# The last block's output: four quarters summed by VectorE out of PSUM and stored as each is ready, the last one from two DMA queues

## The chip, the core and the metric

The kernel runs on one core of a Trainium2 chip. The metric is the device time of one execution in microseconds. The profiler gives, beside that time, the span from the first to the last instruction and a record of every instruction, DMA packet and semaphore. In what follows TensorE is PE (its weight loads are PEld), VectorE is DVE, ScalarE is ACT, GpSimd is POOL and SyncE is SP. SP computes nothing: it issues DMAs.

## The reference

Two stages run one after the other: attention that keeps the 32 largest scores of each row, and a gated feed-forward block on its result.

```python
scores = q @ k.T / sqrt(64)                      # 8 batches, 8 heads, 576 x 576
kth    = 32nd largest of each row
scores = where(scores >= kth, scores, -1e9)
attn   = exp(scores - max); attn /= sum + 1e-9
x      = (attn @ v) as (4608, 512)               # heads side by side
g      = x @ w_gate; val = x @ w_val             # 512 -> 1536
out    = (g * sigmoid(g) * val) @ w_out          # 1536 -> 512, (4608, 512) float32
```

## The kernel before

**Attention** is cut into units, one for a batch, a tile of 128 query rows (64 in the last) and a pair of heads. `scores` multiplies on PE, `select` finds the 32nd largest on DVE by rounds of MAX8 and MATCH_REPLACE8 (L339, L343), `penalize` (L361, POOL) and `weigh` (L370, ACT) form the exponentials, `turn` (L397) transposes them on PE and `values` (L426) multiplies by v. The loop over units at L718 keeps several units in flight and gives the feed-forward work out in pieces between them.

**Feed-forward** work is done in 18 blocks of 256 token rows (`BLK`) by the generator `feed(kb)`. It is ready when the attention rows that it needs are. A block forms `h`, the gated hidden values, in six steps of two 256-wide products each (L480). PE fills a PSUM bank; ACT reads it (L505 to L507, L512); POOL multiplies (L508, L513). When the units are used up, the rest of the work is done by `while piece(): pass` (L775), so the last block runs with no attention beside it.

**The output product** of each block but the first is made with a fast scheme of seven products instead of eight: `quarter(i, ps)` runs the i-th product, six matmul steps at L566 into a PSUM tile of 128 x 256. The order is 1, 7, 5, 6, 2, 4, 3. POOL prepares the operands: L573, L581, L586 and, for quarter 3, L614. `a` (products 5 and 7) and `b` (products 1 and 6) are copies in SBUF, made by ACT at L593 and L600 and summed up on POOL with `tt` (L552, in `sum_up`). The output tile `o` has 128 partitions, two row tiles t = 0 and 1, and 512 columns, so it has four parts of 128 x 256:

- t = 1, right: finished early, from sums of `a` and `b` alone;
- t = 0, left: product 2 plus `b[:, 0]`; ACT copies the bank (L624), POOL adds (L552);
- t = 1, left: product 4 plus `a[:, 1]`;
- t = 0, right: product 3 plus `a[:, 0]`.

Products 4 and 3 go into the two halves of one PSUM tile, `x_ps2`. After product 3, `rest_x` copies both halves by one ACT instruction of 128 x 512 (L636), `stores` adds `a` to both by one POOL instruction of 128 x 512 (L552), and then `store` sends the two row tiles.

`store(o, g0)` (L457) issues DMAs for 128 rows of the output. Since a row of the tile and a row of `out` are not in the same order, it splits the rows where the order breaks; in the last block each row tile gives two DMAs of 64 rows by 2 KB, so the block gives four, all from SP's queue.

**What sets the order.** Copies and POOL sums are put into the lists `on_act` and `on_pool`, and `flush` issues them at places in the loop. At the end every engine's instructions are tied into the order in which they were written (L781 to L794), so each engine runs its own list strictly in that order. PSUM is two pools: five banks for attention and three (`ps_f`) for the feed-forward block, taken in turn.

Of the kernel before, what the change touches and what calls it, by code (L numbers as in the profile page):

```python
# [9 lines left out]
ALU = mybir.AluOpType  # L10
FP32 = mybir.dt.float32
# [4 lines left out]
P = 128  # L16
# [4 lines left out]
BLK = 256  # L21
# [6 lines left out]
def kernel(  # L28
# [37 lines left out]
    nc = tc.nc  # L66
    B, H, S, D = q.shape
    DM, DFF = w_gate.shape
# [8 lines left out]
    NBLK = B * S // BLK  # L77
# [11 lines left out]
    ps_f = ctx.enter_context(tc.tile_pool(name="ps_f", bufs=3, space=PSUM))  # L89
# [355 lines left out]
            done[kb] += n_c  # L445
            at += n_c

    def store(o, g0):

        at = g0  # L450
        while at < g0 + P:
            b, c = divmod(at, S)
            j, p0 = divmod(c, P)
            n = min(g0 + P - at, S - c, P - p0)
            r0 = b * S + (c if j == J else J * p0 + j)
            dst = out[r0 : r0 + n, :] if j == J else out[r0 : r0 + J * (n - 1) + 1 : J, :]
            nc.sync.dma_start(dst, o[at - g0 : at - g0 + n, :])  # L457
            at += n

    on_act, on_pool = [], []  # L460

    def flush(queue):
        while queue:
            queue.pop(0)()

    def feed(kb):
# [50 lines left out]
        o = ffn.tile([P, 2, DM], FP32, tag="o", name="o", bufs=1)  # L517
        if plain:
            for t in range(2):
                ps = ps_f.tile([P, DM], FP32, tag="f", name="o_ps")  # L520
                for m in range(MC):
                    need(4 * MS + m + 1)
                    if m == 6:
                        flush(on_act)
                        flush(on_pool)
                    nc.tensor.matmul(  # L526
                        ps[:],
                        hs[m // 2][:, m % 2, t * P : (t + 1) * P],
                        wo[:, m, :],
                        start=(m == 0),  # L530
                        stop=(m == MC - 1),
                    )
                    if m == MC - 1:

                        def finish(ps=ps, t=t):
                            nc.scalar.copy(o[:, t, :], ps[:])
                            store(o[:, t, :], kb * BLK + t * P)

                        on_act.append(finish)
                        if t == 1:  # L540
                            plain_done.append(True)
                    if m % 2 == 1:
                        yield 1
            return
        while len(T[3]) < MQ:
            next(weight)
        DH = DM // 2
        y_ps = ps_f.tile([P, 2, DH], FP32, tag="f", name="y_ps")
        x_ps = ps_f.tile([P, 2, DH], FP32, tag="f", name="x_ps")

        def tt(out, in0, in1):
            nc.gpsimd.tensor_tensor(out, in0, in1, ALU.add)  # L552

        def quarter(i, ps):
            for m in range(MQ):
                s, r = m // 2, m % 2
                lhsT = {
                    1: lambda: hs[s][:, r, first],
                    2: lambda: hs[s + MS // 2][:, r, first],
                    3: lambda: hs[s][:, r, late],  # L560
                    4: lambda: hs[s + MS // 2][:, r, late],
                    5: lambda: hs[s][:, r, late],
                    6: lambda: s32[:, m],
                    7: lambda: s32[:, m],
                }[i]()
                nc.tensor.matmul(  # L566
                    ps, lhsT, T[i][m], start=m == 0, stop=m == MQ - 1
                )
                if m % 3 == 2:
                    yield 0.75  # L570
# [19 lines left out]
        a = ffn.tile([P, 2, DH], FP32, tag="gv", name="p57", bufs=3)  # L590
# [6 lines left out]
        b = ffn.tile([P, 2, DH], FP32, tag="gv", name="p16", bufs=3)  # L597
# [22 lines left out]
        y_ps2 = ps_f.tile([P, DH], FP32, tag="f", name="y_ps")  # L620
        yield from quarter(2, y_ps2[:])

        def rest_y():
            nc.scalar.copy(o[:, 0, 0:DH], y_ps2[:])  # L624
            on_pool.append(lambda: tt(o[:, 0, 0:DH], o[:, 0, 0:DH], b[:, 0]))

        on_act.append(rest_y)
        x_ps2 = ps_f.tile([P, 2, DH], FP32, tag="f", name="x_ps")
        yield from quarter(4, x_ps2[:, 1])
# [5 lines left out]
        def rest_x():  # L635
            nc.scalar.copy(middle, x_ps2[:])  # L636

            def stores():
                tt(middle, middle, a[:])
                for t in range(2):  # L640
                    store(o[:, t, :], kb * BLK + t * P)

            on_pool.append(stores)
# [7 lines left out]
    def piece():  # L651

        if len(on_act) > 1:
            flush(on_act)
        if len(on_pool) > 1:
            flush(on_pool)
        while True:
            if not current:
                if not todo or done.get(todo[0], 0) < NHP * BLK:
                    return 0  # L660
                flush(on_act)
                flush(on_pool)
                current.append(feed(todo.pop(0)))
            cost = next(current[0], 0)
            if cost == 0:
                current.pop()
                continue
            return cost
# [156 lines left out]
```

## Time and profile before

| | |
|---|---|
| median of 4 runs | 1838.76 us (1837.98 to 1840.82) |
| the profiled execution | 1839.38 us |
| its span | 1837.6 us |
| PE busy | 1707.3 us, 93% of the span |
| DVE, ACT, POOL busy | 88%, 65%, 55% of the span |
| DMA | 59.65 MB, mean 32 GB/s |
| mean granted TensorE clock | 0.964 |

The profiled execution's own time is 1.8 us more than its span. In the rows of the profile, `L566` is a line of the kernel, an `x12` behind a row is the number of instructions merged into it, and `[4.81 <-PE x_ps L566]` says that the engine had stood idle for 4.81 us until a PE instruction of that line ended. A `q` behind an engine's name (`SPq`) is its sequencer: there a DMA issue, a drain or a semaphore wait takes its time.

### The profile page before, as it was taken

What the parts mean: (1) busy time and instruction counts of PE and PEld (TensorE: products, weight loads), DVE (VectorE), ACT (ScalarE), POOL (GpSimd) and SP (SyncE); (2) the same over time, 40 slices, a digit from 0 to 9 for tenths busy, and PEclk for the clock granted to TensorE, in tenths of its full rate; (3) what the DMA queues carried; (4) which work ended last, traced back from release to release, by engine and by line L of the source; (5) the groups of instructions that cost most, each with busy time, mean ns of one, the idle gap of its engine ahead of it and who ended that gap; (6) DMA issues with size and microseconds to landing.
All of it is one profiled execution on the core that took longest, in us unless ns stands there. A gap on an engine that the chain in (4) does not pass through costs nothing.

```text
span 1837.6 us, 30517 instructions
## 1 busy us (share of the span) xinstructions
PE 1707.3 (93%) x10756; PEld 1409.0 (77%) x10756; DVE 1620.8 (88%) x3405; ACT 1202.7 (65%) x2943; POOL 1012.4 (55%) x932
## 2 busy tenths in 40 slices
PE   3438989899999989999999999999999999999998
PEld 2326668777788878887888878888788878888887
DVE  7999999999999879997999989998999989998400
ACT  5667776677666667676767676767776766675431
POOL 3556746645555545655464646564556554646444
PEclk7678999999999999999999999999999999999999
DMA  7322221000300021000300012000300011000000
GB/s 188 97 85 92 59 66 26 12 1 18 77 1 12 1 67 27 12 1 14 73 19 1 13 40 54 1 12 2 74 19 12 1 36 32 1 12 12 1 13 12
DMA packets 109145, 59.65 MB, mean 32 GB/s; under 512 B 88512, under 2 KB 96704, under 8 KB 108992
## 3 DMA queue, kind: packets, MB, share of 16 engines
q1 hardware_dynamic: 107936, 57.44, 12.1%
q8 instruction: 85, 1.39, 0.3%
q14 instruction: 68, 0.56, 0.1%
q10 hardware_dynamic: 1056, 0.26, 0.1%
HBM read 48.23 MB, written 9.44 MB: 31 GB/s over the span
## 4 chain that ended last, share of the span: by engine, by line
PE 82%; DVE 3%; POOL 2%; ACT 2%; issue 2%; DMA 0%; POOLq 0%; ACTq 0%; SPq 0%
PE f L480 39%; PE x_ps L566 9%; PE av L426 8%; PE etps L397 7%; PE s L318 7%; PE y_ps L566 6%; PE s L304 2%; PE av L417 1%; DVE m L339 1%; PE kqps L273 1%; DVE rest L343 1%; PE o_ps L526 1%; POOL e L361 1%; POOL p L552 0%; ACT e L370 0%
## 5 line engine op out<-in xcount | busy, mean ns | idle before, releaser
L339 DVE MAX8 m<-rest 128x8 f32<-128x576 f32 x864 | 613.6, 745 | 2.2
L361 POOL TENSOR_TENSOR e<-e,sc 128x1152 f32<-128x1152 f32 (+1 forms) x160 | 382.7, 2392 | 78.4 <-DVE e L349 72.7
L343 DVE MATCH_REPLACE8 rest<-m,rest 128x576 f32<-128x576 f32 x576 | 423.5, 741 | 0.0
L480 PE MATMUL f<-xT,wg 128*128 128x256 f32 x1728 | 401.6, 382 | 0.0
L480 PE MATMUL f<-xT,wv 128*128 128x256 f32 x1728 | 399.1, 382 | 0.0
L480 PEld LDWEIGHTS f<-xT,wg 128*128 128x128 f32 x1728 | 323.0, 190 | 62.6 <-issue 21.0
L480 PEld LDWEIGHTS f<-xT,wv 128*128 128x128 f32 x1728 | 324.4, 190 | 58.8 <-issue 16.3
L508 POOL TENSOR_TENSOR h<-h,half_g 128x512 f32<-128x512 f32 x108 | 138.1, 1279 | 295.8 <-ACT h L507 295.5
L339 DVE MAX8 m<-sc 128x8 f32<-128x576 f32 x288 | 205.1, 748 | 106.2 <-ACT sc L309 57.8
L370 ACT ACTIVATE e<-e,bias 128x576 f32<-128x576 f32 x288 | 222.1, 776 | 85.9 <-POOL e L361 85.7
L397 PE MATMUL etps<-ident,e 128*128 128x128 f32 (+1 forms) x1312 | 185.1, 286 | 98.8 <-issue 41.0
L398 ACT COPY et<-etps 128x512 f32<-128x512 f32 (+1 forms) x448 | 184.3, 484 | 127.8 <-PE etps L397 126.8
L397 PEld LDWEIGHTS etps<-ident,e 128*128 128x128 f32 (+1 forms) x1312 | 159.5, 147 | 126.2 <-issue 47.0
L513 POOL TENSOR_TENSOR h<-h,val 128x512 f32<-128x512 f32 x108 | 139.9, 1295 | 188.4 <-ACT val L512 188.3
L385 ACT ACTIVATE e<-e,tot 128x576 f32<-128x576 f32 x288 | 211.8, 788 | 7.7 <-DVE tot L382 7.4
L343 DVE MATCH_REPLACE8 rest<-m,sc 128x576 f32<-128x576 f32 x288 | 211.7, 741 | 0.0
L318 PE MATMUL s<-kqT 64*128 64x288 f32 x1024 | 173.6, 450 | 5.1 <-ACT kqT L278 3.2
L349 DVE TENSOR_SCALAR e<-sc,m 128x576 f32<-128x576 f32 x288 | 171.6, 632 | 3.4
L426 PE MATMUL av<-et,v 128*64 128x128 f32 (+1 forms) x2560 | 172.1, 280 | 0.0
L323 ACT COPY sc<-s 128x288 f32<-128x288 f32 x512 | 164.0, 402 | 2.4 <-PE s L318 2.4
L426 PEld LDWEIGHTS av<-et,v 128*64 128x64 f32 x2560 | 135.3, 143 | 22.7 <-issue 6.8
L505 ACT ACTIVATE h<-f 128x512 f32<-128x512 f32 x108 | 65.3, 605 | 132.1 <-PE f L480 132.1
(71 smaller groups left out, 2000.3 us busy)
## 6 DMA issues: line engine op xcount, KB each, us to landing
v<-in_v_dram SPq DMA_DIRECT2D x32, 256.0 KB, 3.0
kq_in<-in_k_dram SPq DMA_DIRECT2D x63, 128.0 KB, 3.0
kq_in<-in_q_dram SPq DMA_DIRECT2D x63, 128.0 KB, 3.1
w<-in_moe_w_gate_dram SPq DMA_DIRECT2D x12, 512.0 KB, 3.8
w<-in_moe_w_val_dram SPq DMA_DIRECT2D x12, 512.0 KB, 3.8
w<-in_moe_w_out_dram SPq DMA_DIRECT2D x12, 512.0 KB, 3.7
out_dram<-o SPq DMA_DIRECT2D x40, 128.0 KB, 2.4
out_dram<-o SPq DMA_DIRECT2D x16, 256.0 KB, 2.4
```

The lines of the kernel that those rows point to most:

```text
L318: nc.tensor.matmul(ps[:, 0:half], slab[d, q0 : q0 + P], slab[d, k0 : k0 + half])
L339: nc.vector.max(m[:, t, 8 * r : 8 * r + 8], cur[:, hs])
L343: nc.vector.match_replace(rest[:, hs], m[:, t, 8 * r : 8 * r + 8], cur[:, hs], LOWEST)
L349: nc.vector.tensor_scalar(e[:, hs], sc[:, hs], m[:, t, TOP_K - 1 : TOP_K], FAR, ALU.is_lt, ALU.mult)
L361: nc.gpsimd.tensor_tensor(e[:, every], e[:, every], sc[:, every], ALU.add)
L370: nc.scalar.activation(e[:, hs], e[:, hs], AF.Exp, bias=bias[:, t : t + 1], scale=scale, accum_out=tot[:, t : t + 1],)
L385: nc.scalar.mul(e[:, hs], e[:, hs], tot[:, t : t + 1])
L397: nc.tensor.transpose(ps[0:kl, c * P : (c + 1) * P], e[:, k0 : k0 + kl], ident[:])
L398: nc.scalar.copy(et[0:kl, c0 : c0 + cn, :], ps[0:kl, 0 : cn * P].rearrange("p (c j) -> p c j", c=cn),)
L426: nc.tensor.matmul(av[hh * R : (hh + 1) * R, 0:ql], v_last[:, hh, :] if c == J else vt[:, hh, c, :], moving, start=last and c == 0, stop=c ...
L480: nc.tensor.matmul(ps[:, i, :], w[:, kc, m * P : (m + 1) * P], x[:, kc, :], start=(kc == 0), stop=(kc == KC - 1),)
L566: nc.tensor.matmul(ps, lhsT, T[i][m], start=m == 0, stop=m == MQ - 1)
```

## The change

In the last block alone (`kb == NBLK - 1`) the way from product 2 on is another one. DVE adds each product, read from its PSUM bank, to its part of `b` or `a` and writes the sum to `o`. Products 4 and 3 get a PSUM tile each. The stores follow each sum: the left half of row tile 0 after product 2 (two DMAs of 64 rows by 1 KB), the whole row tile 1 after product 4 (two of 64 rows by 2 KB), the right half of row tile 0 after product 3 (two of 64 rows by 1 KB, the first issued by ACT and the second by SP). All other blocks do what they did.

```diff
-    def store(o, g0):
+    def store(o, g0, cols=slice(0, DM), queues=(nc.sync,)):
...
-            nc.sync.dma_start(dst, o[at - g0 : at - g0 + n, :])
+            queues[0].dma_start(dst[:, cols], o[at - g0 : at - g0 + n, cols])
+            queues = queues[1:] + queues[:1]
...
         yield from quarter(2, y_ps2[:])
 
+        left, right = slice(0, DH), slice(DH, DM)
+        if kb == NBLK - 1:
+
+
+            flush(on_act)
+            flush(on_pool)
+            g0 = kb * BLK
+            nc.vector.tensor_tensor(o[:, 0, left], y_ps2[:], b[:, 0], ALU.add)
+            store(o[:, 0], g0, left)
+            for i, t, cols in ((4, 1, left), (3, 0, right)):
+                ps = ps_f.tile([P, DH], FP32, tag="f", name="x_ps")
+                yield from quarter(i, ps[:])
+                nc.vector.tensor_tensor(o[:, t, cols], ps[:], a[:, t], ALU.add)
+                if t == 1:
+                    store(o[:, 1], g0 + P)
+                else:
+                    store(o[:, 0], g0, cols, (nc.scalar, nc.sync))
+            return
+
         def rest_y():
-            nc.scalar.copy(o[:, 0, 0:DH], y_ps2[:])
-            on_pool.append(lambda: tt(o[:, 0, 0:DH], o[:, 0, 0:DH], b[:, 0]))
+            nc.scalar.copy(o[:, 0, left], y_ps2[:])
+            on_pool.append(lambda: tt(o[:, 0, left], o[:, 0, left], b[:, 0]))
```

Each engine's instruction order is the same as before up to this place. At the end of the program ACT loses two copies and gains a DMA issue, POOL loses two sums, DVE gains three sums, and SP issues five DMAs where it issued four.

## The prediction

> **What bounds the kernel now.** I read the page's chain first. PE carries 82% of what ended last, so over most of the span only PE's work counts, and the edit touches none of it: its matmuls stay the same in number, size and order. The second line is PE's share by slice.
>
> ```profile
> PE 82%; DVE 3%; POOL 2%; ACT 2%; issue 2%; DMA 0%; POOLq 0%; ACTq 0%; SPq 0%
> PE   3438989899999989999999999999999999999998
> ```
>
> Then the chain of the last microseconds, the only place that can move. Columns are start, length and what. The last matmul ends at 1828.96 + 1.31 = 1830.27; the span ends at 1837.6. So 7.33 us follow the last matmul.
>
> ```profile
> 1828.96 1.31 PE x_ps L566 x6
> 1830.27 0.02 issue
> 1830.30 0.59 ACT o L636
> ...
> 1831.00 1.29 POOLq L820
> ```
>
> The chain stops at POOL because it follows no DMA. The timeline of the same stretch goes on (start, length, engine, line, operation), and also shows what POOL and ACT do beside quarters 2, 4 and 3.
>
> ```profile
> 1824.73 1.27 POOL L552 TENSOR_TENSOR p<-p,p 128x512 f32<-128x512 f32 x1
> 1824.92 2.75 PE L566 MATMUL x_ps<-t,h 128*128 128x256 f32 x12
> 1825.12 0.37 ACT L624 COPY o<-y_ps 128x256 f32<-128x256 f32 x1 [1.95 <-PE y_ps L566]
> 1825.95 2.10 POOL L614 TENSOR_TENSOR h<-h,xT 128x256 f32<-128x256 f32 x3
> 1827.29 2.56 PEld L566 LDWEIGHTS x_ps<-wo,h 128*128 128x128 f32 x12
> 1827.51 2.75 PE L566 MATMUL x_ps<-wo,h 128*128 128x256 f32 x12
> 1828.00 0.73 POOL L552 TENSOR_TENSOR o<-o,p 128x256 f32<-128x256 f32 x1
> 1830.30 0.58 ACT L636 COPY o<-x_ps 128x512 f32<-128x512 f32 x1 [4.81 <-PE x_ps L566]
> 1831.02 1.26 POOL L552 TENSOR_TENSOR o<-o,p 128x512 f32<-128x512 f32 x1 [2.29 <-ACT o L636]
> 1832.31 2.38 SPq L457 DMA_DIRECT2D out_dram<-o  x4
> ```
>
> Last, the four stores by themselves (issue length min/median/max, first and last start, time to landing), SP's wait for them, and SP's closing instructions.
>
> ```profile
> L457 SPq DMA_DIRECT2D out_dram<-o x4: 467/594/596, 1832.3 to 1834.1; - x4
> DMA to landing us min/median/max: 2.3/2.4/2.4
> SPq L820 <- DMA out_dram<-o: 1.8, 1, 1.8
> L820 SPq EVENT_SEMAPHORE  x7: 17/27/28, 1836.5 to 1837.5; - x7
> ```
>
> The 7.33 us are four terms. From the matmul to the first store: 0.03 + ACT 0.59 + 0.13 of hand-over + POOL 1.26 + 0.03 = 2.04 (1830.27 to 1832.31). From the first store's issue to the fourth's: 1.79 (to 1834.10). The fourth's landing: 2.4 (to 1836.5). The closing waits and barrier: 1.1 (to 1837.6). 2.04 + 1.79 + 2.4 + 1.1 = 7.33.
>
> **The change part by part.**
>
> *The ACT copy and POOL sum behind quarter 3 become one DVE sum.* No row shows DVE reading PSUM, nor a floating-point two-tensor sum on it. The nearest is the two-tensor operation of L130 on 128x512: median 0.672 us. Small DVE operations give the fixed part: the 128x2 reciprocal took 0.154. So 256 columns cost 0.154 + (0.672 - 0.154)/2 = 0.41. Bounds: 0.37, ACT's copy of the same shape (L624), and 0.67, the whole of L130. I take 0.41, since the form is L130's. First term: 0.03 + 0.41 + 0.03 = 0.47 in place of 2.04, a gain of 1.57 (1.3 to 1.6).
>
> *The queue of four issues becomes one issue on each of two queues.* SP's other four are out of the way. Quarter 2 ends at about 1825.08, its sum at 1825.52, and two issues at up to 0.64 from start to start end by 1826.8. Quarter 4 ends near 1827.68, its sum at 1828.12, two issues end by 1829.4, 1.3 before 1830.74, when the last sum is done; they land by 1831.2, ahead of the last. If SP were late by more than 1.3, the second term would come back. ACT's last work before its issue is the copy L600, done at 1823.16, so nothing stands behind ACT's wait for DVE's semaphore but its closing drain. The second term goes from 1.79 to 0: a gain of 1.79. Without the second queue it would be 0.64.
>
> *The landing of the last pair.* Each DMA has 64 rows of 1 KB rather than 2 KB, and two run at once. Only the kernel's first microsecond shows two queues at once: ACT's and SP's loads issued at 0.72 landed after 2.7 and 3.4, SP's 0.7 later. But these move 512 pieces of 256 B each, not 64. Below stands the 16 KB load of a corner of v, 2.0. Bounds 2.0 and 3.4; I take 2.3, that of the first of the four stores, which like these meets an idle queue and has 64 pieces; the pair carries the same 128 KB as that one. Against the fourth store's 2.4 a gain of 0.1 (from 0.4 gained to 1.0 lost). The Trainium skill's page "DMA: Bandwidth & Descriptors", section "Issuing engines are not separate DMA queues", speaks against expecting much: DMAs of all issuers run on the same 16 engines and interleave, and a second issuer saves only sequencer time. By that rule the pair keeps the 0.64 of issue and gains nothing in transfer, so the sum would stay as I have it; by the start's row it would lose 0.7.
>
> *The first two DVE sums beside POOL.* They run at 1825.1 and 1827.7, under PE's quarters 4 and 3, and take ACT's 0.37 and POOL's 0.73 off engines that were not late: no gain. They could hold POOL back, whose three L614 are what quarter 3 waits for. These end at 1826.65, 1827.35 and 1828.05; the weights of quarter 3 are loaded from 1827.29, with the next pair of steps each 0.86 later (by the chain a quarter takes 2.59, so a third of that), so their slack is 0.64, 0.80 and 0.96. A full block of 0.41 by the first sum, and 0.82 by both before the third, fits. The longest L130 took 1.21, with POOL at work; a block of that length would cost 1.21 - 0.64 = 0.6. I take 0, bound 0.6. The Trainium skill ("SBUF — State Buffer", "Who interferes with whom") would have no block at all, as each sum has only one input in SBUF; no row of before shows this form.
>
> *Waits.* Before its first sum DVE waits for the eight lanes of earlier stores; those were issued by 1770.0 and landed within 3.9, and DVE's last work, a reciprocal, ended at 1764.6: nothing. Nobody is queued behind it. The PSUM tiles of quarters 4 and 3 are the banks that ACT's copies L600 and L593 freed at 1823.16 and 1820.57, before quarter 4 starts: nothing.
>
> *The end.* The closing waits stay: 1.1.
>
> New sum: 0.47 + 0 + 2.3 + 1.1 = 3.87 in place of 7.33, so 3.46 less. The profiled execution would go from 1839.38 to 1835.92 (its span to 1834.1). It lies 0.62 above the median of the runs shown; from the median, 1838.76 - 3.46 = 1835.3.
>
> **The rivals.** The measurement can tell about 0.2%, 3.7 us, from no change.
>
> *A, as summed:* 3.5 off, 1835.3 (0.19%), just short of 0.2%.
>
> *B, two queues are no quicker than one:* the second lands 0.64 to 0.7 later, like the start's pair. 3.46 - 0.67 = 2.8 off: 1836.0. For it: the only pair on record; against it: that pair has eight times as many pieces.
>
> *C, half-size pieces land sooner:* 2.0 rather than 2.3, and one closing wait of the five fewer behind the landing: 3.8 to 3.9 off, 1834.9, past 0.2%. For it: the fall from 3.0 for loads of 128 KB to 2.0 for 16 KB; against it: 256 KB stores land in the same 2.4 as 128 KB ones.
>
> *D, part of the gain is eaten by POOL or a slow PSUM read:* 0.6 late by a blocked L614, and 0.26 if the sum takes 0.67: 2.6 off, 1836.2; with B's loss, 1.9 off, 1836.8.
>
> *E, slower:* ACT's queue has carried no DMA since its second issue at 1.39. If its first one after so long were slow, everything waits for it. It must land 2.3 + 3.5 = 5.8 after its issue to undo the gain and 9.4 to be 0.2% slower; the slowest load from that queue took 3.7. That nothing changes is no case: the instruction lists at the end do differ.
>
> **How the numbers follow.** A 0.45, B 0.22, C 0.15, D 0.15, E 0.03. The four runs of before spread by 2.8, so a median of some runs is uncertain by about half a microsecond to one; A is 0.2 short of the 0.2% bound, and I give 0.4 of it to the far side. Faster: 0.18 of A, 0.12 of C, 0.03 of B and D, 0.33 in all. Slower: 0.02, from E. The same: 0.65. Range: from C with half a microsecond of run noise, 1834.2, to the worst of D with the same, 1837.3.
>
> **What would show it.** Right: in the changed profile the last matmul still ends near 1830.3; a DVE sum of about 0.41 follows it by 0.03; one DMA issue each on ACT and SP starts within 0.1 of its end; and 3.9 us lie between the last matmul and the span's end. A: both land near 2.3. B: SP's lands 0.6 or more after ACT's. C: both under 2.1. D: PE idle ahead of quarter 3, or the sum at 0.6 or more. Wrong altogether: SP still issuing row tile 1 at 1830.7, a landing over 4 from ACT's queue, or a matmul end that has moved by a microsecond, which would be none of these steps.

## The result and the profile after

The changed kernel took 1835.74 us in the median of 36 runs (1834.37 to 1837.93), the kernel before 1839.35 us in 56 runs beside them (1837.88 to 1841.85): 3.61 us less. The ratio is 0.998, with a 95% interval of 0.9975 to 0.9985. The interval lies wholly below 1, so it is faster, clear of the measurement. The gain is 0.196%, just short of the 0.2% that the prediction had named as the border. The profiled execution took 1834.57 us with a span of 1832.8.

The views below are those that the prediction read. Lines of the code have moved by one (L566 is now L567, L614 is L615); L631 and L636 are the sums on VectorE (DVE). First the chain on the page, then the end of the chain (start, length, what), and last the same two quarters in the chain of the kernel before.

```profile
PE 80%; DVE 6%; POOL 2%; ACT 2%; issue 2%; DMA 0%; POOLq 0%; DVEq 0%; ACTq 0%
```

```profile
1823.83 5.19 PE x_ps L567 x24
1829.02 0.02 issue
1829.05 0.42 DVE o L636
```

```profile
1825.08 5.19 PE x_ps L566 x24
```

PE's share of the chain on the page is 80% here and 82% before; e2 below, with the instructions of the kernel before up to the last stores, has 80% and e10 83%, so that difference is variation. Quarters 4 and 3 take 5.19 as before, so TensorE (PE) was not held up. One DVE sum stands where ACT's copy and POOL's sum stood. The timeline of the same stretch (start, length, engine, line, operation, idle time before it):

```profile
1823.47 1.27 POOL L553 TENSOR_TENSOR p<-p,p 128x512 f32<-128x512 f32 x1
1823.92 0.42 DVE L631 TENSOR_TENSOR o<-y_ps,p 128x256 f32<-128x256 f32 x1 [60.53 <-PE y_ps L567]
1824.37 5.59 SPq L457 DMA_DIRECT2D out_dram<-o  x5
1824.70 2.10 POOL L615 TENSOR_TENSOR h<-h,xT 128x256 f32<-128x256 f32 x3
1826.53 0.42 DVE L636 TENSOR_TENSOR o<-x_ps,p 128x256 f32<-128x256 f32 x1 [2.18 <-PE x_ps L567]
1829.05 0.42 DVE L636 TENSOR_TENSOR o<-x_ps,p 128x256 f32<-128x256 f32 x1 [2.10 <-PE x_ps L567]
1829.50 0.56 ACTq L457 DMA_DIRECT2D out_dram<-o  x1
```

The sums run at 0.42 beside POOL, whose 1.27 and 2.10 are what they were before. SP's row merges five issues; the fifth starts with ACT's at 1829.50. The last two stores by themselves: each queue's issue and the time to landing of the two (min/median/max), then ACT's alone, then the waits of SP:

```profile
L457 SPq DMA_DIRECT2D out_dram<-o x1: 467/467/467, 1829.5 to 1829.5; - x1
L457 ACTq DMA_DIRECT2D out_dram<-o x1: 556/556/556, 1829.5 to 1829.5; - x1
DMA to landing us min/median/max: 2.0/2.1/2.2
```

```profile
L457 ACTq DMA_DIRECT2D out_dram<-o x1: 556/556/556, 1829.5 to 1829.5; - x1
DMA to landing us min/median/max: 2.2/2.2/2.2
```

```profile
SPq L457 <- DVE o L636: 2.7, 2, 1.4
SPq L840 <- DMA out_dram<-o: 1.7, 1, 1.7
```

SP waited for DVE up to 1.4 at a time: its queue was free. The last of its earlier stores landed 0.85 after the last matmul, ahead of both of the pair. The landing of ACT's store is the last event before the closing waits.

In what follows the **tail** is the time from the end of the last matmul to the end of the span, by the trace's records to a hundredth. It was 7.30 before (7.33 in the prediction's rounded rows) and is 3.78 now, 3.53 less (7.304 and 3.775). In the two profiled executions the last matmul also ends 1.25 apart (1830.27 and 1829.02); over all the profiles of this study it ends between 1828.9 and 1832.6 where PE's work is the same, so that part is variation from run to run (up to the change, each engine's records stand in the same order in both), and the tail tells the kernels apart better than the median does. Each tail is read from one trace. Pieces that two kernels share agree to about 0.05 or better: the first store after quarter 2 landed 1.95 after its issue in each of the six that have it as the change does.

### The profile page after: what moved, and what is told of

Read it like the earlier page. It is cut to its first block, busy times and chain, and to the rows that moved or that the text cites. A ratio compares the mean times of both kernels' runs of the same rounds, so it can differ in the third digit from the quotient of the medians.

```text
span 1832.8 us, 30525 instructions
## 1 busy us (share of the span) xinstructions
PE 1703.3 (93%) x10756; PEld 1405.2 (77%) x10756; DVE 1623.1 (89%) x3408; ACT 1201.5 (66%) x2941; POOL 1011.0 (55%) x930
## 4 chain that ended last, share of the span: by engine, by line
PE 80%; DVE 6%; POOL 2%; ACT 2%; issue 2%; DMA 0%; POOLq 0%; DVEq 0%; ACTq 0%
PE f L481 39%; PE x_ps L567 9%; PE av L426 7%; PE etps L397 7%; PE s L318 7%; PE y_ps L567 6%; DVE m L339 2%; DVE rest L343 2%; PE s L304 2%; PE av L417 1%; PE kqps L273 1%; PE o_ps L527 1%; POOL e L361 1%; DVE e L349 1%; POOL p L553 0%
## 5 line engine op out<-in xcount | busy, mean ns | idle before, releaser
L339 DVE MAX8 m<-rest 128x8 f32<-128x576 f32 x864 | 613.6, 745 | 2.2
L339 DVE MAX8 m<-sc 128x8 f32<-128x576 f32 x288 | 205.1, 748 | 104.3 <-ACT sc L309 58.4
```

The source lines that it names most:

```text
L339: nc.vector.max(m[:, t, 8 * r : 8 * r + 8], cur[:, hs])
```

## The experiments

Each is the changed kernel with one edit, or the kernel before with one; the diffs show it. The fourth column is the way from the last matmul to the last issue, that store's landing, and what follows the landing; each is rounded by itself, so a row can miss its tail by 0.01.

| kernel | tail | first store of the last group issued after the last matmul | last issue, its landing, rest | median, with ratio to before |
|---|---|---|---|---|
| before | 7.30 | 2.05 | 3.84 + 2.37 + 1.09 | 1839.35 |
| changed | 3.78 | 0.49 | 0.49 + 2.24 + 1.04 | 1835.74, 0.998 |
| e1, one queue | 4.03 | 0.49 | 1.00 + 2.07 + 0.96 | 1836.57, 0.9983 (0.9974 to 0.9992) |
| e2, two queues alone | 6.68 | 2.05 | 2.64 + 3.03 + 1.02 | 1838.96, 0.9997 (0.9988 to 1.0006) |
| e3, sums, whole rows last | 4.53 | 0.49 | 1.00 + 2.42 + 1.11 | 1837.57, 0.9986 (0.9977 to 0.9995) |
| e4, stores alone | 4.79 | 1.24 | 1.75 + 2.07 + 0.97 | 1837.00, 0.9988 (0.9979 to 0.9997) |
| e5, ACT's half only | 3.59 | 0.49 | 0.49 + 2.05 + 1.04 | one run |
| e6, queues swapped | 3.88 | 0.49 | 0.49 + 2.34 + 1.04 | one run |
| e7, whole rows last, two queues | 4.23 | 0.49 | 0.49 + 2.65 + 1.08 | one run |
| e8, sums from SBUF | 4.18 | 0.89 | 0.90 + 2.24 + 1.04 | one run |
| e9, every block | 3.68 | 0.49 | 0.49 + 2.22 + 0.97 | 1846.64, 1.0038 (1.0024 to 1.0052) |
| e10, one sum alone | 6.12 | 0.85 | 2.64 + 2.38 + 1.10 | 1839.08, 0.9993 (0.9984 to 1.0002) |
| e11, further lanes | 3.74 | 0.49 | 0.49 + 2.34 + 0.90 | 1836.68, 0.9980 (0.9971 to 0.9989) |
| e12, further lanes, halves kept | 3.62 | 0.49 | 0.50 + 2.22 + 0.90 | 1836.01, 0.9982 (0.9973 to 0.9991) |

The medians with several rounds agree in size with the tails where the difference is large, and say nothing on differences of a few tenths.

### e1: the last pair from one queue

```diff
-                    store(o[:, 0], g0, cols, (nc.scalar, nc.sync))
+                    store(o[:, 0], g0, cols)
```

> The last pair of stores goes out from SP alone. What is read is the tail, from the last matmul's end to the span's end: 7.33 us before, 3.78 with the whole change. Theory (issue and landing add up): the second issue starts about 0.52 after the first, as the first pair's did, and lands 2.1 after that, so at 2.6 in place of ACT's 2.25: tail 4.1, time some 0.35 above the changed kernel. Rival 1 (the second queue saves a whole issue of 0.64): tail 4.4. Rival 2 (two queues are no quicker than one, ACT's lateness eats the issue saved): tail 3.8 or less.

The tail is 4.03, next to the 4.1 of the theory. SP's two issues and landings:

```profile
L457 SPq DMA_DIRECT2D out_dram<-o x2: 467/532/596, 1830.1 to 1830.6; - x2
DMA to landing us min/median/max: 2.0/2.0/2.1
```

The second issue starts 0.51 after the first and lands at 0.51 + 2.07 = 2.58, where ACT's landed at 2.24. So the second queue wins 0.34 at the landing and 0.25 in the tail, not the 0.64 of a whole issue; the close behind it, 0.96 for 1.04, gives the difference back.

### e2: the two queues without the rest

```diff
-            nc.sync.dma_start(dst, o[at - g0 : at - g0 + n, :])
+            queues[0].dma_start(dst, o[at - g0 : at - g0 + n, :])
+            queues = queues[1:] + queues[:1]
...
-                    store(o[:, t, :], kb * BLK + t * P)
+                    store(
+                        o[:, t, :], kb * BLK + t * P,
+                        (nc.scalar, nc.sync) if kb == NBLK - 1 else (nc.sync,),
+                    )
```

> The kernel before, only with its last four stores issued in turn by ACT and SP. Theory I (the spacing of the issues is what made the four stores late): two issues on each queue, 0.64 between them, landing 2.4: the tail falls from 7.33 to 2.04 + 0.64 + 2.4 + 1.1 = 6.2. Rival T (the sixteen DMA engines are full with 512 KB, and the issues only keep pace with them): the data take as long as before from the first packet on, and the tail stays at 7.0 to 7.3.

Neither number came: the tail is 6.68, halfway. Both queues issue twice, ACT's last at 2.64 after the last matmul where SP's fourth was at 3.84. That is 1.20 earlier. But its landing takes longer:

```profile
L457 ACTq DMA_DIRECT2D out_dram<-o x2: 550/670/791, 1832.5 to 1833.1; - x2
DMA to landing us min/median/max: 2.7/2.9/3.0
L457 SPq DMA_DIRECT2D out_dram<-o x2: 466/531/596, 1832.5 to 1833.0; - x2
DMA to landing us min/median/max: 2.3/2.4/2.5
```

With the four issues, 512 KB in all, starting within 0.59 rather than 1.79, the last landing grows from 2.37 to 3.03 and eats 0.66 of the 1.20. ACT's two stores landed later than SP's by 0.4 and 0.5, so both the sharing and ACT's queue have a part in it; this run does not divide them. The median shows no difference that can be told. A second queue on its own was worth little; what the change did was to send three quarters of the data off before the last product was ready.

### e3: meant as the sums without early stores

```diff
-            store(o[:, 0], g0, left)
             for i, t, cols in ((4, 1, left), (3, 0, right)):
...
-                if t == 1:
-                    store(o[:, 1], g0 + P)
-                else:
-                    store(o[:, 0], g0, cols, (nc.scalar, nc.sync))
+            for t in range(2):
+                store(o[:, t], g0 + t * P)
```

> VectorE's three sums as in the change, but no store before the last sum; then the four whole-row stores of before, from SP. Both theories: only the first term changes, 2.04 to 0.48: tail 0.48 + 1.79 + 2.4 + 1.1 = 5.8, some 1.5 less time than before. If the tail comes out nearer 7, the sum was not on the path.

The tail of 4.53 fits neither reading, since the kernel did not do what it was meant to. The stores of row tile 1 are written behind those of row tile 0, but the trace has them 2.0 and 1.5 before the last matmul's end. SP's row of four issues starts behind the sum of quarter 4, ahead of the last one:

```profile
1829.10 0.42 DVE L635 TENSOR_TENSOR o<-x_ps,p 128x256 f32<-128x256 f32 x1 [2.18 <-PE x_ps L567]
1829.56 3.63 SPq L457 DMA_DIRECT2D out_dram<-o  x4
1831.62 0.42 DVE L635 TENSOR_TENSOR o<-x_ps,p 128x256 f32<-128x256 f32 x1 [2.10 <-PE x_ps L567]
```

The end of the program does not tie every engine's list into the written order, as the section on the kernel before has it: L781 names four engines, and SP is not one of them. Here the two pairs of stores stand in the order in which their data are ready. The run is useful as something else. It is e1 with the left half held back: the last two stores are 64 rows of 2 KB. Against e1 (4.03) whole rows at the end cost 0.50, of which 0.35 is the landing (2.42 for 2.07).

### e4: stores as parts are ready, sums by ACT and POOL

```diff
-            nc.vector.tensor_tensor(o[:, 0, left], y_ps2[:], b[:, 0], ALU.add)
+            nc.scalar.copy(o[:, 0, left], y_ps2[:])
+            tt(o[:, 0, left], o[:, 0, left], b[:, 0])
...
-                nc.vector.tensor_tensor(o[:, t, cols], ps[:], a[:, t], ALU.add)
+                nc.scalar.copy(o[:, t, cols], ps[:])
+                tt(o[:, t, cols], o[:, t, cols], a[:, t])
...
-                    store(o[:, 0], g0, cols, (nc.scalar, nc.sync))
+                    store(o[:, 0], g0, cols)
```

> The stores as each part is ready, from SP alone, but each sum by an ACT copy of 128x256 and a POOL sum of 128x256 as in the other blocks. Theory: 0.02 + 0.37 + 0.13 + 0.73 + 0.03 = 1.28 to the first store of the last pair, then 0.52 + 2.1 + 1.05: tail 4.9 to 5.0, some 2.4 less time than before. Rival: POOL, with L614 and three sums to do in the same microseconds, is late for quarter 3, PE waits, and the last matmul itself comes later.

The tail is 4.79, the theory's 4.9 to 5.0 less 0.1. The rival did not happen: PE's quarter 3 starts 2.60 after quarter 4 (1824.70 and 1827.30) where it was 2.59 before, and POOL is done with L615 in time.

```profile
1825.74 2.09 POOL L615 TENSOR_TENSOR h<-h,xT 128x256 f32<-128x256 f32 x3
1827.30 2.75 PE L567 MATMUL x_ps<-wo,h 128*128 128x256 f32 x12
1827.49 0.37 ACT L637 COPY o<-x_ps 128x256 f32<-128x256 f32 x1 [2.22 <-PE x_ps L567]
1827.79 1.40 POOL L553 TENSOR_TENSOR o<-o,p 128x256 f32<-128x256 f32 x2
1830.09 0.37 ACT L637 COPY o<-x_ps 128x256 f32<-128x256 f32 x1 [2.22 <-PE x_ps L567]
1830.54 0.72 POOL L553 TENSOR_TENSOR o<-o,p 128x256 f32<-128x256 f32 x1 [1.34 <-ACT o L637]
```

Against e1, which differs in the sums alone, the DVE sum is worth 4.79 - 4.03 = 0.76: 0.37 and 0.72 with two hand-overs against 0.42 with one.

### e10: one VectorE sum in the old place

```diff
-            nc.scalar.copy(middle, x_ps2[:])
+            if kb == NBLK - 1:
+                nc.vector.tensor_tensor(middle, x_ps2[:], a[:], ALU.add)
+            else:
+                nc.scalar.copy(middle, x_ps2[:])
...
-                tt(middle, middle, a[:])
+                if kb < NBLK - 1:
+                    tt(middle, middle, a[:])
```

> The kernel before, only with its last ACT copy and POOL sum of 128x512 replaced by one VectorE sum of 128x512 out of the bank; then the four whole-row stores of before, from SP. It is what e3 was to be: there the stores of row tile 1 went out ahead of the last sum all the same. Theory (the four terms add up): first term 0.04 + 0.69 + 0.03 = 0.76 in place of 2.05, the rest as before, 1.79 + 2.37 + 1.09: tail 6.0, 1.3 less. Rival (part of the copy and sum was hidden, or four stores behind a quicker sum meet something else): tail over 6.5.

The tail is 6.12. The sum of 128x512 took 0.69, as L130's 0.672 had let expect:

```profile
1831.27 0.69 DVE L637 TENSOR_TENSOR o<-x_ps,p 128x512 f32<-128x512 f32 x1 [65.71 <-PE x_ps L566]
1832.03 2.39 SPq L457 DMA_DIRECT2D out_dram<-o  x4
```

The four issues behind it take 2.39 as before (2.38), and the terms add up but for the first, 0.85 for 0.76: the sum starts 0.09 after the last matmul where 0.04 was expected, and the store follows it by 0.07 where 0.03 was. With e3, e1 and the changed kernel it makes a ladder: 7.30, one sum 6.12 (1.18 off), three sums with row tile 1 stored before the end 4.53 (1.59 off, 0.36 of it the smaller last sum), the left half stored early too 4.03 (0.50 off), the second queue 3.78 (0.25 off).

### e5, e6, e7: what the last pair's landing is made of

For e5, SP's half is not issued:

```diff
-            queues[0].dma_start(dst[:, cols], o[at - g0 : at - g0 + n, cols])
+            if queues[0] is not None:
+                queues[0].dma_start(dst[:, cols], o[at - g0 : at - g0 + n, cols])
...
-                    store(o[:, 0], g0, cols, (nc.scalar, nc.sync))
+                    store(o[:, 0], g0, cols, (nc.scalar, None))
```

> The changed kernel without SP's half of the last pair, so 64 rows of the right half of row tile 0 are not written: ACT's DMA is alone. With both, ACT's landed 2.24 after its issue and SP's 1.97. Theory (ACT's queue is slower by itself): 2.2 again, tail 3.8. Rival (the two share the DMA engines): ACT's lands at 1.95 to 2.0, as the first store after quarter 2 did alone on SP, tail 3.5.

For e6, the queues the other way round:

```diff
-                    store(o[:, 0], g0, cols, (nc.scalar, nc.sync))
+                    store(o[:, 0], g0, cols, (nc.sync, nc.scalar))
```

> The changed kernel with the last pair's halves given to the other queue each: SP takes the first 64 rows, ACT the second. Theory (the queue makes the difference): ACT's lands last again, 2.2 to 2.3 against 1.95 to 2.0, tail 3.8. Rival (the rows or the order of the two in the program make it): SP's lands last. It is a second look at the tail of the changed kernel too.

For e7, row tile 0 whole at the end:

```diff
-            store(o[:, 0], g0, left)
...
-                    store(o[:, 0], g0, cols, (nc.scalar, nc.sync))
+                    store(o[:, 0], g0, slice(0, DM), (nc.scalar, nc.sync))
```

> The changed kernel without the store after quarter 2: the last pair carries whole rows, two DMAs of 64 rows by 2 KB, on ACT and SP. Theory T (the data's time counts: 256 KB in place of 128 KB on the same sixteen engines): 0.3 to 0.6 later, tail 4.1 to 4.4. Rival (a landing is a fixed latency, whatever the size): tail 3.8.

**e5:** alone, ACT's store lands after 2.05, and the tail is 3.59. That lies between the two and nearer the rival: of the 0.29 by which 2.24 exceeds 1.95, sharing makes 0.19. The rest, 0.10, is put down to the queue: SP's store of the same size, alone after quarter 2, lands after 1.95, and ACT's issue takes 0.56 where SP's first takes 0.47.

**e6:** ACT's lands last again, as the theory had it, but both were later than in the changed kernel: 2.34 and 2.18 for 2.24 and 1.97. So queue and place both count: the two queues differ by 0.06 on the first 64 rows and by 0.37 on the second.

**e7:** with whole rows the tail is 4.23, the lower half of the theory's span. ACT's issue and landing, then SP's:

```profile
L457 ACTq DMA_DIRECT2D out_dram<-o x1: 557/557/557, 1830.4 to 1830.4; - x1
DMA to landing us min/median/max: 2.7/2.7/2.7
L457 SPq DMA_DIRECT2D out_dram<-o x1: 466/466/466, 1830.4 to 1830.4; - x1
DMA to landing us min/median/max: 2.4/2.4/2.4
```

A landing is no fixed latency. For SP alone it was 1.95 with 64 KB and 2.24 with 128 KB; for the last of a pair on two queues 2.24 with 64 KB each and 2.65 with 128 KB each. Halving the last pair's pieces is worth 0.46 of the tail here, 0.41 of it in the landing.

The DMA packets in these traces show where the time of a landing goes. On SP the first packet starts 1.12 after the issue does, and the 64 KB pass in 0.46. ACT's alone (e5) start after 1.21 and pass in 0.46; beside SP's, in the changed kernel, they start after 1.42 and pass in 0.44. So the pair costs ACT's store a later start and not a slower transfer, and ACT's queue too is later by its start. With e6's swap, packets of both queues keep these times to 0.02. What grows there is the time from the last packet to the landing: 0.39 to 0.50 for ACT, 0.39 to 0.60 for SP.

### e8: the sums with both inputs in SBUF

```diff
-            nc.vector.tensor_tensor(o[:, 0, left], y_ps2[:], b[:, 0], ALU.add)
+            nc.scalar.copy(o[:, 0, left], y_ps2[:])
+            nc.vector.tensor_tensor(o[:, 0, left], o[:, 0, left], b[:, 0], ALU.add)
...
-                nc.vector.tensor_tensor(o[:, t, cols], ps[:], a[:, t], ALU.add)
+                nc.scalar.copy(o[:, t, cols], ps[:])
+                nc.vector.tensor_tensor(o[:, t, cols], o[:, t, cols], a[:, t], ALU.add)
```

> Each of the three sums in two steps: ACT copies the bank into the output tile (0.37), VectorE then adds in place, both inputs in SBUF. Tail: 0.37 and a hand-over of 0.05 more, 4.2, if the sum itself stays at 0.42. Rival on VectorE and POOL in each other's way: with two SBUF inputs the first sum, beside POOL's 128x512 sum, or POOL's work beside it, takes up to 0.4 longer than alone; with the slack of 0.6 ahead of quarter 3 PE does not move. If neither grows, POOL and VectorE were never in each other's way here.

The tail is 4.18, the 4.2 expected, and the rival on DVE and POOL shows as well:

```profile
1825.23 1.26 POOL L553 TENSOR_TENSOR p<-p,p 128x512 f32<-128x512 f32 x1
1825.63 0.37 ACT L631 COPY o<-y_ps 128x256 f32<-128x256 f32 x1 [1.95 <-PE y_ps L567]
1826.09 0.69 DVE L632 TENSOR_TENSOR o<-o,p 128x256 f32<-128x256 f32 x1 [60.94 <-ACT o L631]
1826.46 2.27 POOL L615 TENSOR_TENSOR h<-h,xT 128x256 f32<-128x256 f32 x3
1828.69 0.43 DVE L638 TENSOR_TENSOR o<-o,p 128x256 f32<-128x256 f32 x1 [1.91 <-ACT o L637]
```

Beside POOL the first sum takes 0.69, alone the second takes 0.43; POOL's three take 2.27 for 2.10, all of it in the first (0.91 for 0.73). In the changed kernel, where the sum's first input is in PSUM, the same pair of engines at the same place shows 0.42 and 2.10. This is the rule that the prediction weighed, from the Trainium skill's page "SBUF — State Buffer", section "Who interferes with whom": a DVE instruction with at most one SBUF input does not contend with GpSimd outside the two-port modes, one with two does with a GpSimd instruction that reads SBUF. Both halves agree with these runs. PE's quarters 4 and 3 take 5.19 in both, as the slack of 0.6 had let expect.

### e9: the same in every block

```diff
-        if kb == NBLK - 1:
+        if kb >= 1:
```

> The change in every block of the fast scheme, not the last alone. VectorE gets 16 x 3 sums of 0.42, 20 us more, and runs its list in order, so in the stretches with attention its top-k work waits for quarters 2, 4 and 3. Theory: VectorE at 89% has no room for it and PE waits for the units: 1840 to 1860. Rival (PE is the bound, and ACT loses 15 us and POOL 32 us of work): within 2 us of the changed kernel.

It took 1846.64 us, ratio to before 1.0038 (1.0024 to 1.0052): slower than before by 7 us and than the changed kernel by 11. The granted clock does not make it: e9's runs at 0.964 took 1846.2 to 1846.64, the changed kernel's at 0.964 at most 1837.44. The largest waits of DVE between 250 and 1700 us (who waited for whom: us in total, times, longest), and POOL's for DVE's top-k work:

```profile
DVE o L636 <- PE x_ps L567: 24.1, 11, 6.3
DVE o L631 <- ACT e L385: 15.7, 5, 5.0
DVE o L631 <- issue: 15.0, 4, 5.9
DVE m L339 <- ACT sc L309: 6.2, 6, 2.7
POOL e L361 <- DVE e L349: 218.7, 76, 11.2
```

The same of the changed kernel:

```profile
DVE m L339 <- ACT sc L323: 36.4, 28, 2.2
DVE m L339 <- ACT sc L309: 36.3, 12, 8.6
POOL e L361 <- DVE e L349: 50.9, 25, 6.3
```

DVE's idle time has moved: it stood ahead of the top-k work (L339), waiting for new scores, and now stands ahead of the sums, with the top-k work queued behind them. The sums cost 0.42 and waits of up to 6.3 us. POOL, the next stage of the units, waits for DVE four times as long as in the changed kernel. Between 250 and 1000 us PE was busy for 724 us, where in the changed kernel it was 730. So the way that wins at the end, where DVE has nothing else to do, loses where DVE is 89% busy. One further part is not taken apart by a run: e9 also gives ACT a store issue in each block that waits for DVE's last sum, and ACT stood idle for 1.8 to 5.6 us ahead of four of the sixteen added ones.

### e11 and e12: the closing waits

```diff
-                    store(o[:, 1], g0 + P)
+                    store(o[:, 1], g0 + P, right)
+                    store(o[:, 1], g0 + P, left)
```

e11 has in addition the other order of the queues, as in e6; e12 has not.

> The changed kernel with row tile 1 stored as two halves (the right one, ready 5 us earlier, first), so that the last pair's semaphores are the last two that SP's closing waits ask for; the pair's halves change queues. After the changed kernel's last landing three further waits of some 0.065 each stood. Theory: two of them go, tail 3.78 - 0.13 = 3.65, and the two whole-row stores, whose data were under way until 0.5 after the last matmul, are smaller and gone earlier. Rival: the two further DMAs hold SP's queue for another 1.1 and put its half of the last pair late, tail above 3.9. In the median neither shows: 0.1 of 1836 is far below what runs differ by.

> As e11, with the last pair's halves on the queues of the changed kernel (ACT the first 64 rows, SP the second). With the halves swapped ACT's landing took 2.34 in both runs that had it, and 2.22 to 2.24 in the three that had it this way. Theory (the halves' place makes 0.1, repeatably): landing 2.24, then the short close of e11, 0.90: tail 0.49 + 2.24 + 0.90 = 3.63, the shortest. Rival (the 0.1 is chance, or comes with the two further stores): 2.34 again, tail 3.74.

After the last landing SP goes through its remaining waits, and with the pair's semaphores at the end of that list the rest falls from 1.04 to 0.90 in both, as expected. In e11 the swap of the halves cost 0.10 again (landing 2.34); e12 keeps them and has the shortest tail, 3.62 where 3.63 was expected. SP's further stores held nothing up. In the median (1836.01, ratio 0.9982) e12 can't be told from the changed kernel.

## Why the prediction was right

**The bound.** As forecast, only the tail moved. Quarters 4 and 3 took 5.19 before and after, and PE's busy share is 93% in both.

**First term**, 2.04 to 0.47: 2.05 to 0.49. The sum took 0.42 where 0.41 had been interpolated from L130 and the reciprocal; reading PSUM cost nothing that shows. e4 and e10 show the term by itself.

**Second term**, 1.79 to 0: so it was (0.00 between SP's issue and ACT's). SP had been idle for 1.4 when the last sum came, where 1.3 was reckoned. The aside that it "would be 0.64" without the second queue was mis-sized: the spacing is 0.51 after a pause, the second landing is shorter than ACT's, and the queue is worth 0.25 in the tail (e1).

**Third term**, landing 2.3: 2.24. That the number held was in part luck: it was taken from a store of 64 rows by 2 KB, and two effects that the sum left out nearly cancel. The half-size pieces land sooner (1.95 alone on SP), which was rival C; and the second queue and the sharing put 0.3 on top (0.10 the queue, 0.19 the sharing, by e5), a mild form of rival B, with ACT's store the late one and not SP's. By the signs that the prediction set, with landings of 1.97 and 2.24, neither A (both near 2.3) nor B (SP's 0.6 later) nor C (both under 2.1) came out as it stood. The kernel's first microseconds, with 0.7 between two queues, overstated B. The other page of the Trainium skill that was weighed, "DMA: Bandwidth & Descriptors", section "Issuing engines are not separate DMA queues", says that a second issuer saves sequencer time alone, as the transfers share the engines. e2 agrees in direction: 1.20 of issue saved, 0.66 lost in the landing; of what the issue saved, 0.54 was kept up to the landing.

**Fourth term**, 1.1: 1.04, from 1.09. Four waits rather than five stood behind the last landing, a part of rival C that the sum of A had left out.

**POOL and the waits**, costed at nothing: POOL's three L615 took 2.10, and DVE's list of waits ended in time. Sum: 3.46 forecast, 3.53 in the tails, 3.61 in the medians. The forecast of 1835.3 lies 0.4 below 1835.74, since the median of the kernel before was 0.6 higher in the longer series.

**Rivals D and E** did not occur: no block of L615, no late queue (2.24, not 5.8).

**The chances.** By the border of 0.2% the gain falls just short, as A had it. But with 36 and 56 runs the interval (0.15% to 0.25% off) does not reach down to nothing, so these runs tell even less than 0.2% from no change. The 0.65 given to "the same" against 0.33 for "faster" rested on the wider border. The lower end of the range is a slip: C less half a microsecond is 1834.4, not 1834.2.

**One of the tests named was wrong:** a matmul end moved by a microsecond was to mean that something else had happened. It moved by 1.25 (to 1829.02), and by more among kernels with the same PE work. The tail, not the place of the last matmul, was the thing to watch.

## What to carry to other kernels

What follows the last matmul is bare time: read it as a sum of hand-overs, issues, landing and close, and take work out of it by doing early all that is ready early, and by sending the data off in parts so that the last transfer is small. Use for the last step the engine that does it in one instruction and has nothing else to do then; the same instruction in the middle of the kernel, where that engine is busy and its list is in order, came with 11 us more than the changed kernel takes. A second queue for the last stores adds a little; on its own, with all the data still to go, it gave back over half of what it saved (0.66 of 1.20).

## What the runs showed of the hardware that was not expected

- Which half of the last pair goes to which queue makes 0.1, repeatably: 2.22 to 2.24 for ACT's landing in four runs with the first 64 rows on ACT, 2.34 in the two with them on SP. The packets end at the same time to 0.02 in e6 and e11; the difference stands between the last packet and the landing. Why is open; the halves differ in their partitions and in their rows of the output.
- A store of 64 rows by 1 KB alone on ACT's queue took 0.56 to issue and 2.05 to land (e5) where SP's took 0.47 and 1.95.
- Each wait that SP still has to go through behind the last landing costs about 0.065, though it is long fulfilled: moving two of them ahead of the landing was worth 0.13 to 0.14 (e12, e11).
